# The second weight 32 bytes further in the on-chip memory

## The chip, the cores and the metric

The kernel runs on one core of a Trainium2 chip. A core has a matrix engine (PE; the loading of its stationary operand is shown as a row of its own, PEld), three engines that work on vectors (DVE, ACT and POOL), a queue engine (SP) that starts transfers, an on-chip memory of 128 partitions from which all engines read, and a small accumulation memory into which PE writes. The metric is the time of one execution in microseconds as the device reports it; lower is better. A time is the median of several executions.

## The reference

Two steps follow each other. The first is a windowed attention over 8 batches and 8 heads: 512 local positions that see 32 neighbours on either side and 32 global positions, and the 32 global positions that see everything.

```python
s_g = scale * np.matmul(q_g, k_all.transpose(0, 1, 3, 2))
out_g = np.matmul(sm(s_g), v_all)
mask = np.abs(pos[:, None] - pos[None, :]) <= window
s_ll = np.where(mask, scale * np.matmul(q_l, k_l.transpose(0, 1, 3, 2)), -1e9)
s_lg = scale * np.matmul(q_l, k_g.transpose(0, 1, 3, 2))
out_l = np.matmul(sm(np.concatenate([s_lg, s_ll], axis=-1)), np.concatenate([v_g, v_l], axis=2))
```

Its result, 4352 rows of 512 values, goes through a feed-forward layer with 2048 hidden values:

```python
h = x @ w_in
r = np.maximum(h, 0.0)
g = s * (r * r) + b
return (g @ w_out).astype(np.float32)
```

## The kernel before

Every float32 operand of a product is split into a rounded part and the rest, and a product is computed as three (rounded by rounded, rounded by rest, rest by rounded). So both weights lie in the on-chip memory twice, rounded part and rest: `wi` (line 109) and `wo` (line 110), each 65,536 bytes in every partition. They are loaded in 32 pieces at the start (`weight_piece`): a piece is decoded by ACT and DVE and written with one ACT copy (line 156, the rounded part) and one DVE subtraction (line 157, the rest).

The work is a loop over j. In round j the kernel computes the attention of head slot j (scores at line 355, the scores of the global positions at line 359, transposes at line 308, products with the values at line 380; now and then the global part at lines 428 and 451) and, ten rounds behind, one eighth of the feed-forward layer of 256 rows: `ffn_in` (line 499) and, a round later, `ffn_out` (line 532). There are 17 row tiles of 256 rows, so 136 such eighths. From j = 20 on the order of PE's instructions is the order in which the code stands.

An eighth is 24 products in `ffn_in`, each with a 128x128 piece of `wi` as the stationary operand and 256 columns of the tile `xs` as the moving operand, and 12 products in `ffn_out`, each with a 128x128 piece of the tile `g` as the stationary operand and 512 columns of `wo` as the moving operand:

```python
nc.tensor.matmul(
    oacc[t][i], lhsT=g[:, a, k, i * P:(i + 1) * P], rhs=wo[:, e, f, :],
    start=(pr == 0 and n == 0), stop=(pr == 7 and n == 5),
)
```

PE loads the stationary operand of the next product while the moving operand of the present one streams, so two reads of the on-chip memory go on at a time. Where the tiles lie is decided when the program is built. In bytes modulo 256, of the start in each partition:

| tile | role on PE | place modulo 256 before |
|---|---|---|
| `wi` | stationary, line 499 | 0 |
| `xs` | moving, line 499 | 32 |
| `g` (2 buffers) | stationary, line 532 | 0, 0 |
| `wo` | moving, line 532 | 0 |
| `kq` (3 buffers, used in turn) | stationary and moving, line 355 | 192, 224, 0 |
| `vs`, `pt` (2 buffers each) | stationary and moving, line 380 | 32 |

All pieces that PE reads of `wi`, `wo`, `g` and of the queries in `kq` start at a multiple of 512 bytes from the start of their tile, so they have the tile's place modulo 256.

Of the kernel before, what the change touches and what calls it, by code (L numbers as in the profile page):

```python
# [11 lines left out]
F32R = mybir.dt.float32r  # L12
# [8 lines left out]
DM, DF = 512, 2048  # L21
P = 128
# [45 lines left out]
def window_attention_then_ffn(ctx: ExitStack, tc: tile.TileContext, qd, qp, qg, kw, vw, vg, w_in, w_out, sv, bv, out):  # L68
# [3 lines left out]
    const = ctx.enter_context(tc.tile_pool(name="const", bufs=1))  # L72
# [34 lines left out]
        masks[first] = mask  # L107

    wi = const.tile([P, 2, 4, DF], F32R, name="wi")
    wo = const.tile([P, 2, 16, DM], F32R, name="wo")  # L110

    xg_d = dram.tile([B * SG, DM], F32, name="xg_d")

# [591 lines left out]
```

## Time and profile before

| | |
|---|---|
| median of 3 runs | 1034.99 us (1034.93 to 1036.73) |
| profiled execution, its own time | 1035.21 us |
| its span, first to last instruction | 1033.4 us |
| granted PE clock over the span | 0.979 |
| PE busy | 998.6 us (97%) |
| DVE, ACT, POOL busy | 813.8, 710.4, 300.2 us |
| line 499 (`ffn_in`) | 3264 products of 256 columns |
| line 532 (`ffn_out`) | 1632 products of 512 columns |

In the profile a PE row is a product, a PEld row the load of a stationary operand. Products are pipelined: the recorded duration of one is longer than the time from its start to the start of the next, and their ends are modelled, so durations of PE rows overlap. What a product costs is read from the starts, or from how its duration differs from that of another of the same shape.

### The profile page before, as it was taken

The page shows a single profiled execution, that of the slowest core. Times are in us where ns is not written, and L with a number is a line of the kernel's source. Part 1 is how long each engine was busy: PE and PEld are TensorE (multiplying, and loading weights), DVE is VectorE, ACT ScalarE, POOL GpSimd, SP SyncE. Part 2 cuts the span into 40 slices and gives each one's busy share as a digit, 9 for nine tenths or more (in the row PEclk, how much of TensorE's full clock was granted, in tenths as well). Part 3 has the DMA queues.
Part 4 walks back from the last instruction along what each step waited for, and adds up shares of the span by engine and source line. Part 5 has one row for each costly group of instructions (what it writes and reads, how often), then busy time and mean ns, then how long its engine had stood idle before and what let it go on. Part 6 is the DMA issues. An engine that isn't in the chain of part 4 may idle for free.

```text
span 1033.4 us, 20334 instructions
## 1 busy us (share of the span) xinstructions
PE 998.6 (97%) x7060; PEld 904.7 (88%) x7060; DVE 813.8 (79%) x2096; ACT 710.4 (69%) x1816; POOL 300.2 (29%) x365
## 2 busy tenths in 40 slices
PE   7779989999999999999999999999999999999996
PEld 3468879999999999999999999998999989999995
DVE  6999878888888988888888888888888888873321
ACT  6998767777676777777677777777677777643221
POOL 0000443333333433333323433344323433111000
PEclk8789989999999999999999999999999999999998
DMA  8764232222221222223221222222222321101000
GB/s 301 248 219 151 89 91 73 72 59 90 88 73 54 72 87 76 79 61 90 74 79 56 77 83 67 79 67 87 75 75 58 95 72 44 43 24 35 12 21 21
DMA packets 62254, 85.73 MB, mean 83 GB/s; under 512 B 7368, under 2 KB 49352, under 8 KB 62152
## 3 DMA queue, kind: packets, MB, share of 16 engines
q1 hardware_dynamic: 61864, 83.39, 26.1%
q8 instruction: 56, 0.92, 0.4%
q10 hardware_dynamic: 288, 1.05, 0.3%
q14 instruction: 46, 0.38, 0.1%
HBM read 74.97 MB, written 9.44 MB: 82 GB/s over the span
## 4 chain that ended last, share of the span: by engine, by line
PE 85%; ACT 5%; DVE 5%; DMA 3%; issue 1%; SPq 0%; DVEq 0%; ACTq 0%
PE ps_h L499 34%; PE acc L532 34%; PE ps_t L308 5%; PE ps_o L380 4%; PE ps_s L355 4%; PE ps_og L451 2%; DMA wst<-in_w_out 2%; PE ps_g L359 1%; ACT sm L219 1%; ACT wst L147 1%; DVE g L514 1%; DVE x L393 1%; DMA b_t<-in_bv 1%; DVE r L506 1%; ACT g L513 1%
## 5 line engine op out<-in xcount | busy, mean ns | idle before, releaser
L499 PE MATMUL ps_h<-xs,wi 128*128 128x256 f32 x3264 | 419.3, 284 | 0.0
L532 PE MATMUL acc<-wo,g 128*128 128x512 f32 x1632 | 405.0, 395 | 0.5 <-ACT g L513 0.5
L499 PEld LDWEIGHTS ps_h<-xs,wi 128*128 128x128 f32 x3264 | 397.1, 190 | 3.3 <-issue 0.5
L532 PEld LDWEIGHTS acc<-wo,g 128*128 128x128 f32 x1632 | 294.9, 188 | 56.8 <-ACT g L513 0.8
L514 DVE SCALAR_TENSOR_TENSOR g<-r,b_t,g 128x512 fp32r<-128x512 f32 x136 | 120.3, 885 | 57.6 <-ACT g L513 57.0
L505 ACT ACTIVATE r<-ps_h 128x512 f32<-128x512 f32 x136 | 81.3, 598 | 115.5 <-PE ps_h L499 109.7
L513 ACT ACTIVATE g<-r,b_t 128x512 fp32r<-128x512 f32 x136 | 98.4, 723 | 78.6 <-DVE r L506 78.1
L192 POOL TENSOR_TENSOR kq<-rq,kq 128x256 fp32r<-128x256 f32 x112 | 83.9, 750 | 231.1 <-ACT kq L191 226.7
L506 DVE SCALAR_TENSOR_TENSOR r<-ps_h,s_t,r 128x512 f32<-128x512 f32 x136 | 101.2, 744 | 58.3 <-ACT r L505 58.3
L190 POOL TENSOR_TENSOR kq<-rk,kq 64x416 fp32r<-64x416 f32 x56 | 61.0, 1089 | 264.3 <-ACT kq L189 254.4
L219 ACT ACTIVATE sm<-sm,nm 128x224 f32<-128x224 f32 (+1 forms) x256 | 119.7, 469 | 1.4 <-DVE nm L213 1.0
L200 POOL TENSOR_TENSOR vs<-rv,vs 128x256 fp32r<-128x256 f32 x112 | 91.2, 815 | 51.2 <-ACT vs L199 45.9
L308 PE MATMUL ps_t<-ident,sm 128*128 128x128 f32 (+1 forms) x512 | 96.8, 277 | 7.9 <-DVE pg L433 3.0
L363 ACT COPY tg<-ps_g 32x256 f32<-32x256 f32 (+1 forms) x112 | 42.3, 378 | 72.3 <-PE ps_g L359 71.7
L380 PE MATMUL ps_o<-pt,vs 128*128 128x256 f32 x448 | 91.0, 285 | 0.0
L213 DVE CUSTOM_DVE_ANT_0 sm<-ps_s,mask 128x192 f32<-128x192 f32 (+1 forms) x224 | 74.6, 370 | 11.2 <-PE ps_s L355 11.0
L443 POOL TENSOR_TENSOR vsg<-rvg,vsg 128x320 fp32r<-128x320 f32 x64 | 57.8, 924 | 77.5 <-ACT vsg L442 77.5
L391 DVE TENSOR_TENSOR u<-ps_o,u 128x256 f32<-128x256 f32 x112 | 47.3, 422 | 41.8 <-ACT u L390 40.0
L355 PE MATMUL ps_s<-kq 128*128 128x192 f32 (+1 forms) x448 | 78.4, 266 | 0.0
L355 PEld LDWEIGHTS ps_s<-kq 128*128 128x128 f32 x448 | 72.0, 190 | 6.8
L308 PEld LDWEIGHTS ps_t<-ident,sm 128*128 128x128 f32 (+1 forms) x512 | 58.4, 145 | 13.3 <-ACT ptp L315 4.6
L228 DVE TENSOR_SCALAR sm<-sm,ss 128x192 f32<-128x192 f32 (+1 forms) x224 | 68.0, 346 | 1.0
(83 smaller groups left out, 1239.2 us busy)
## 6 DMA issues: line engine op xcount, KB each, us to landing
rq<-in_qd SPq DMA_DIRECT2D x112, 128.0 KB, 2.3
rv<-in_vw SPq DMA_DIRECT2D x112, 128.0 KB, 2.1
rk<-in_kw SPq DMA_DIRECT2D x56, 208.0 KB, 2.4
rvg<-in_vg SPq DMA_DIRECT2D x32, 320.0 KB, 2.9
out<-o SPq DMA_DIRECT2D x34, 256.0 KB, 2.0
wst<-in_w_in SPq DMA_DIRECT2D x15, 512.0 KB, 4.3
wst<-in_w_out SPq DMA_DIRECT2D x15, 512.0 KB, 4.3
rvp<-in_vw SPq DMA_DIRECT2D x8, 256.0 KB, 3.5
```

Of the source, the lines that this page charges most:

```text
L192: nc.gpsimd.tensor_sub(out=qs[:, 1, :], in0=rq, in1=f32(qs[:, 0, :]))
L200: nc.gpsimd.tensor_sub(out=vs[:, :, 1, :], in0=rv4, in1=f32(vs[:, :, 0, :]))
L219: nc.scalar.activation(out=p, in_=p, func=AF.Exp, bias=nm[:, n:n + 1], scale=-1.0, accum_out=ss[:, n:n + 1],)
L308: nc.tensor.transpose(out=p_t[:, at:at + q], in_=sm[0:q, c0:c0 + P], identity=ident[0:q, 0:q])
L355: nc.tensor.matmul(p_s[:, cols], lhsT=qs[:, a, blk * P:(blk + 1) * P], rhs=ks[:, cols], start=(a == 0), stop=(a == 1),)
L380: nc.tensor.matmul(p_o[:, blk, :, q0:q0 + n], lhsT=vs[:, 2 * blk + c], rhs=pt[:, :, o], start=(c == 1), stop=(c == 0),)
L499: nc.tensor.matmul(p_h[:, k], lhsT=wi[:, a, c, f * P:(f + 1) * P], rhs=xs[:, e, c, :], start=(n == 0), stop=(n == 11),)
L505: nc.scalar.activation(out=r, in_=p_h, func=AF.Relu)
L506: nc.vector.scalar_tensor_tensor(out=r, in0=p_h, scalar=s_t, in1=r, op0=ALU.mult, op1=ALU.mult)
L513: nc.scalar.activation(out=g[:, 0], in_=r, func=AF.Identity, bias=b_t)
L514: nc.vector.scalar_tensor_tensor(out=g[:, 1], in0=r, scalar=b_t, in1=f32(g[:, 0]), op0=ALU.add, op1=ALU.subtract,)
L532: nc.tensor.matmul(oacc[t][i], lhsT=g[:, a, k, i * P:(i + 1) * P], rhs=wo[:, e, f, :], start=(pr == 0 and n == 0), stop=(pr == 7 and n == 5),)
```

## The change

`wo` is taken as 32 * 512 + 64 elements instead of 32 * 512, and its view starts 8 elements (32 bytes) into that.

```diff
-    wo = const.tile([P, 2, 16, DM], F32R, name="wo")
+    wo = const.tile([P, 32 * DM + 64], F32R, name="wo")
+    wo = wo[:, 8:32 * DM + 8].rearrange("p (a f d) -> p a f d", a=2, f=16)
```

In the built program `wo` itself now starts at 32 modulo 256. All tiles that are placed behind it (`kq`, `xs`, `g` and the rest) move by 256 bytes, so they keep their places modulo 256; `wi` and what lies before it do not move at all. The instructions of all five engines and the semaphores that they wait for stand in the same order as before, row by row. `ffn_in` and `ffn_out` read and compute the same values.

## The prediction

> **What bounds the kernel now.** I read the page's busy times and the chain of waits first, then the busy times by stretch.
>
> ```profile
> PE 998.6 (97%) x7060; PEld 904.7 (88%) x7060; DVE 813.8 (79%) x2096; ACT 710.4 (69%) x1816; POOL 300.2 (29%) x365
> PE 85%; ACT 5%; DVE 5%; DMA 3%; issue 1%; SPq 0%; DVEq 0%; ACTq 0%
> PE ps_h L499 34%; PE acc L532 34%; PE ps_t L308 5%; PE ps_o L380 4%; PE ps_s L355 4%; PE ps_og L451 2%; DMA wst<-in_w_out 2%; PE ps_g L359 1%; ACT sm L219 1%; ACT wst L147 1%; DVE g L514 1%; DVE x L393 1%; DMA b_t<-in_bv 1%; DVE r L506 1%; ACT g L513 1%
> 413.00:517.00 104.00, 103.50 (x762) 96.17 (x761) 87.73 (x234) 75.90 (x202) 38.09 (x45) 1.00 0.26 76
> L499 PE MATMUL ps_h<-xs,wi 128*128 128x256 f32 x3264 | 419.3, 284 | 0.0
> L532 PE MATMUL acc<-wo,g 128*128 128x512 f32 x1632 | 405.0, 395 | 0.5 <-ACT g L513 0.5
> ```
>
> The fourth row is a stretch of the steady stage: PE busy 103.5 of 104 us at the full granted clock (1.00), DVE 87.7, ACT 75.9, POOL 38.1. PE is the bound, the two feed-forward lines are two thirds of the chain, and L532, the only line that reads `wo` on PE, hardly ever waits (0.5 us in all). The next engine, DVE, has 16 us in 104 free. So whatever a product of L532 gets longer or shorter, up to many times what is in question here, goes into the end of the program one to one.
>
> How long is a product? The timeline of PE near the end, where no attention is left, shows it:
>
> ```profile
> 1004.82 2.96 PE L499 MATMUL ps_h<-xs,wi 128*128 128x256 f32 x24
> 1007.62 2.91 PE L532 MATMUL acc<-wo,g 128*128 128x512 f32 x12
> 1010.37 2.96 PE L499 MATMUL ps_h<-xs,wi 128*128 128x256 f32 x24
> ```
>
> The 12 products of L532 take 1010.37 - 1007.62 = 2.75 us, 229 ns each. Their recorded durations, first five and last seven of the same run:
>
> ```profile
> L532 PE MATMUL acc<-wo,g 128*128 128x512 f32 x5 | 1.3, 393 | 0.0
> L532 PE MATMUL acc<-wo,g 128*128 128x512 f32 x7 | 1.7, 389 | 0.0
> ```
>
> The mean is (5 x 393 + 7 x 389) / 12 = 390.7 ns, so a recorded duration is the true pace plus some 161 ns, and differences between durations are differences in pace. The five vary, and the last seven are equal:
>
> ```profile
> L532 PE MATMUL acc<-wo,g x5: 389/393/398, 1007.6 to 1008.5; 128*128 128x512 f32 x5
> L532 PE MATMUL acc<-wo,g x7: 389/389/389, 1008.8 to 1010.1; 128*128 128x512 f32 x7
> ```
>
> So the same instruction on the same kind of data takes 389 to 398 ns, with no other engine in the way: after some unsettled products the run falls into a quiet state at 389 (a pace of 227) and stays there. An ordinary product of L532 now has a mean of about 391 (another run, in the steady stage, shows the same); the 395 of the whole line holds the few that follow a wait or a transpose.
>
> ```profile
> L532 PE MATMUL acc<-wo,g 128*128 128x512 f32 x11 | 2.7, 390 | 0.0
> ```
>
> **The change part by part.** No instruction is added, removed or moved, and no wait. What remains is where bytes lie.
>
> First, the loads: the 16 ACT copies and 16 DVE subtractions into `wo` write at another place. The same two instructions into `wi` are the nearest rows:
>
> ```profile
> L157 DVE TENSOR_TENSOR wo<-we,wo 128x512 fp32r<-128x512 f32 x16 | 10.9, 688 | 1.0 <-ACT wo L156 1.0
> L157 DVE TENSOR_TENSOR wi<-we,wi 128x512 fp32r<-128x512 f32 x15 | 10.2, 683 | 0.0
> L156 ACT CAST wo<-we 128x512 fp32r<-128x512 f32 x16 | 9.8, 620 | 2.6 <-DVE we L152 2.5
> L156 ACT CAST wi<-we 128x512 fp32r<-128x512 f32 x15 | 9.3, 617 | 0.1
> ```
>
> These engines took no notice of which weight it was (5 and 3 ns apart). I take nothing; even 5 ns on all 32 with no cover is 0.16 us, either sign.
>
> Second, the tiles behind `wo` move by 256 bytes. Where two of them meet on PE their distance stays; towards `wi`, which does not move, it changes by 256. That everything depends on places modulo 256 at most is an assumption; I take nothing here and leave the failure to the range.
>
> Third, the term that matters: 1632 products read `wo` from 32 instead of 0 modulo 256 while the next piece of `g`, at 0, is loaded. Does PE care how the moving and the stationary operand lie to each other? The trace of before holds an experiment on it. At the end of most eighths, the last product of L532 streams `wo` (at 0) while the first stationary operand of L355 is loaded from one of the three `kq` buffers, at 0, 192 or 224 modulo 256. There are 37 such ends for each buffer. First and last of the 37, the duration of that one product, for the buffer at 0, then 192, then 224:
>
> ```profile
> L532 PE MATMUL acc<-wo,g x1: 389/389/389, 112.3 to 112.3; 128*128 128x512 f32 x1
> L532 PE MATMUL acc<-wo,g x1: 389/389/389, 894.4 to 894.4; 128*128 128x512 f32 x1
> L532 PE MATMUL acc<-wo,g x1: 388/388/388, 117.5 to 117.5; 128*128 128x512 f32 x1
> L532 PE MATMUL acc<-wo,g x1: 388/388/388, 901.3 to 901.3; 128*128 128x512 f32 x1
> L532 PE MATMUL acc<-wo,g x1: 397/397/397, 125.7 to 125.7; 128*128 128x512 f32 x1
> L532 PE MATMUL acc<-wo,g x1: 396/396/396, 908.2 to 908.2; 128*128 128x512 f32 x1
> ```
>
> A stationary operand at 224 costs the product 7 to 8 ns over one at 0 or 192. And 224 is 32 below the next 256: the moving operand lies 32 past the stationary one, modulo 256. That is exactly how `wo` at 32 will lie to `g` at 0, for every pair of products in `ffn_out`. So the first estimate is an ordinary mean of 396 instead of 391: 1632 x 5 ns = 8.2 us.
>
> What it does not tell is how the next product goes on. A product that took longer starts the next at another moment, and the unsettled rows above show that this matters. If the offset only takes the quiet state away, a product costs what the unsettled ones do now, 393 by the five of that run: 1632 x (393 - 391) = 3.3 us. I take the middle, 394.5: 1632 x 3.5 ns = **5.7 us**.
>
> Bounds on the other side: if the new offset has a quiet state too and a run falls into it at once, every ordinary product takes 388 to 389: 1632 x 2 to 3 ns, a gain of 3.3 to 4.9 us.
>
> Nearest to the new pairing in another shape is L499, moving operand `xs` at 32 against `wi` at 0:
>
> ```profile
> L499 PE MATMUL ps_h<-xs,wi x24: 277/279/283, 1004.8 to 1007.5; 128*128 128x256 f32 x24
> L499 PE MATMUL ps_h<-xs,wi x3264: 274/280/582, 46.0 to 1018.6; 128*128 128x256 f32 x192
> ```
>
> It settles, but at 279 to 280, while the line's fastest is 274 ns, 5 below its median. L532 with its operands at 0 and 0 settles at 389, over a minimum of 387. That speaks, weakly, for a dearer settled state at the new offset: 3 to 5 ns dearer than 389 is 392 to 394, 1.6 to 4.9 us in all. It is weak, since in L499 a load of the same size has half as long to hide.
>
> The Trainium skill says the opposite. "SBUF — State Buffer", section "Who interferes with whom", gives PE two independent read ports, one for the moving operand and one for the loading of weights, and says that PE and ACT never wait on anyone; by it the sum is nothing and the time stays 1035.2 us. The trace disagrees: the three buffers give 389, 388 and 396 ns in the same position.
>
> The sum: 1035.2 (the profiled execution, span 1033.4 and 1.8 around it) + 5.7 = 1040.9, say 1041 us. The median of the runs shown is 0.2 us below the profiled execution, which is less than the estimate can tell.
>
> **The rivals.**
>
> Rival A, no change. The runs of `ffn_out` unsettle and settle as they do now, only at another moment: the mean stays within 1 ns of 391, under 1.7 us. For it: the 12 products start from whatever L499 left, and already now a run is a mixture. Against: 7 ns in the one pairing that was tried, nearly every time. Time 1035, up to 2 us either way. The page named above would have this outcome too, by another reason.
>
> Rival B, faster. With `wo` at 32 against `g` at 0, L532 gets the same offset between its operands as L499, so that going from one line to the other no longer unsettles the run: every product at 388 to 389, the first five too. For it: the unsettled products stand at the start of a run, just behind L499. Against: the 396 at this offset. Time 1035.2 - 3.3 to 4.9, about 1031.
>
> Rival C, slower still: each product pays the full price of the pairing seen, 396 to 397, and never settles: 1632 x 5 to 6 ns = 8 to 10 us, 1043 to 1045. It is my own case at its end, and stands inside it.
>
> That the change doesn't do what it says can be left out: the built program has `wo` at 32.
>
> **How the numbers follow.** Slower, with C: 0.55. No change: 0.2. Faster: 0.25, as the pairing was seen only for one product after another offset, and a quiet state at the new one is quite possible. Less than 0.2% (2 us) can't be told from no change. The likeliest case by itself is 1038 to 1045. The range reaches to the faster rival, since that has a quarter: 1031 to 1045.
>
> **What would show it.** In the profile after, the median of L532 tells it: 393 to 397 with me, 389 with no change, 389 with a mean under 393 for the whole line with rival B. The row of L499 should stay at 284, since its operands keep their places modulo 256; if it moves, that assumption was wrong. The last product before L355 should change partners: slow with the `kq` buffer at 0 (moving 32 past stationary), quick with the one at 224. I am wrong if the 12 products settle within two or three of a start, at 389 or less.

## The result and the profile after

The change makes the kernel slower: the median goes from 1034.96 us (6 runs, 1034.61 to 1036.73) to 1040.66 us (6 runs, 1040.00 to 1043.00), a ratio of 1.0052 with a 95% interval of 1.0039 to 1.0065. The profiled execution took 1040.02 us, with a span of 1038.2 us against 1033.4, 4.8 us more.

Busy times, the steady stretch and the two feed-forward lines of the changed kernel (its lines stand one further down: 500 is 499 of before, 533 is 532):

```profile
PE 1004.9 (97%) x7060; PEld 905.1 (87%) x7060; DVE 814.7 (78%) x2096; ACT 710.0 (68%) x1816; POOL 300.7 (29%) x365
413.00:517.00 104.00, 103.57 (x753) 95.41 (x752) 87.98 (x234) 75.09 (x199) 37.27 (x44) 1.00 0.25 76
L500 PE MATMUL ps_h<-xs,wi 128*128 128x256 f32 x3264 | 419.8, 284 | 0.0
L533 PE MATMUL acc<-wo,g 128*128 128x512 f32 x1632 | 410.9, 398 | 0.8 <-ACT g L514 0.8
```

PE is busy 6.3 us longer, and 5.9 of that is in line 533 (405.0 before). DVE, ACT and POOL are within 1 us of before, line 500 is where it was (419.3 and 284 ns), and the granted clock is 1.00 in the stretch in both. The products of `ffn_out` alone have become longer.

A run near the end shows how. Timeline of PE of the changed kernel, then the distribution (shortest, median, longest) of the durations of products 6 to 11 of one run, first in the changed kernel (line 533) and then in the kernel before (line 532):

```profile
1009.51 2.96 PE L500 MATMUL ps_h<-xs,wi 128*128 128x256 f32 x24
1012.32 2.96 PE L533 MATMUL acc<-wo,g 128*128 128x512 f32 x12
1015.12 1.09 PE L500 MATMUL ps_h<-xs,wi 128*128 128x256 f32 x8
L533 PE MATMUL acc<-wo,g x6: 393/395/397, 1002.3 to 1003.4; 128*128 128x512 f32 x6
L532 PE MATMUL acc<-wo,g x6: 389/389/389, 1003.2 to 1004.4; 128*128 128x512 f32 x6
```

The 12 products take 1015.12 - 1012.32 = 2.80 us, 233 ns each in place of 229. The six that stood at 389 before now differ from neighbour to neighbour: from start to start the run goes 234, 231, 235, 233, 234, 231, 235, ... ns to its end. The quiet state at 227 ns has gone, and not in this run alone: in the trace of before, 98 of the 136 runs come to four neighbours within 2 ns of each other, at 226 to 227; in the trace after, none does. For the whole line:

```profile
L533 PE MATMUL acc<-wo,g x1632: 388/396/505, 70.8 to 1029.0; 128*128 128x512 f32 x182
L500 PE MATMUL ps_h<-xs,wi x3264: 274/280/583, 45.6 to 1023.4; 128*128 128x256 f32 x192
```

The median went from 389 to 396. Reading every start of the line from the two traces, and leaving out the some 70 products that follow a wait or a transpose (over 245 ns), the mean time from start to start is 229.5 ns before and 233.2 after: 3.7 ns more on 1560 products, 5.8 us. The intervals of the line as a whole, waits and all, add up to 380.4 us before and 385.5 after.

### The profile page after: what moved, and what is told of

Read it like the earlier page. It is cut to its first block, busy times and chain, and to the rows that moved or that the text cites. A ratio compares the mean times of both kernels' runs of the same rounds, so it can differ in the third digit from the quotient of the medians.

```text
span 1038.2 us, 20334 instructions
## 1 busy us (share of the span) xinstructions
PE 1004.9 (97%) x7060; PEld 905.1 (87%) x7060; DVE 814.7 (78%) x2096; ACT 710.0 (68%) x1816; POOL 300.7 (29%) x365
## 4 chain that ended last, share of the span: by engine, by line
PE 81%; DVE 8%; ACT 5%; DMA 3%; issue 2%; ACTq 0%; DVEq 0%
PE acc L533 33%; PE ps_h L500 33%; PE ps_t L309 4%; PE ps_o L381 4%; PE ps_s L356 4%; DMA wst<-in_w_out 2%; PE ps_og L452 1%; DVE g L515 1%; DMA wst<-in_w_in 1%; ACT sm L220 1%; PE ps_g L360 1%; DVE x L394 1%; DVE sm L229 1%; DVE r L507 1%; ACT wst L148 1%
## 5 line engine op out<-in xcount | busy, mean ns | idle before, releaser
L533 PE MATMUL acc<-wo,g 128*128 128x512 f32 x1632 | 410.9, 398 | 0.8 <-ACT g L514 0.8
L515 DVE SCALAR_TENSOR_TENSOR g<-r,b_t,g 128x512 fp32r<-128x512 f32 x136 | 119.8, 881 | 57.6 <-ACT g L514 57.2
L193 POOL TENSOR_TENSOR kq<-rq,kq 128x256 fp32r<-128x256 f32 x112 | 83.9, 749 | 232.8 <-ACT kq L192 228.3
```

The source lines that it names most:

```text
L193: nc.gpsimd.tensor_sub(out=qs[:, 1, :], in0=rq, in1=f32(qs[:, 0, :]))
L515: nc.vector.scalar_tensor_tensor(out=g[:, 1], in0=r, scalar=b_t, in1=f32(g[:, 0]), op0=ALU.add, op1=ALU.subtract,)
L533: nc.tensor.matmul(oacc[t][i], lhsT=g[:, a, k, i * P:(i + 1) * P], rhs=wo[:, e, f, :], start=(pr == 0 and n == 0), stop=(pr == 7 and n == 5),)
```

## The experiments

In all of them the instructions of every engine stand in the same order as in the kernel before, and the values computed are the same; only places in the on-chip memory differ. The edits are shown by their main lines; declarations and loads that go with them are left out. Ratios are taken against executions of the kernel before that were measured beside each experiment (medians 1034.20 to 1035.77 us). "Pace" is the time from the start of a product to the start of the next, in ns, read from the trace; products that follow a wait or a transpose are left out of its means.

Two theories were to be told apart. **R**: what counts is how the moving and the stationary operand lie to each other, modulo 256 (their distance). **M**: what counts is where the moving operand itself lies.

### The 256 bytes alone

```diff
-    wo = const.tile([P, 2, 16, DM], F32R, name="wo")
+    wo = const.tile([P, 32 * DM + 64], F32R, name="wo")
+    wo = wo[:, 0:32 * DM].rearrange("p (a f d) -> p a f d", a=2, f=16)
```

> The second weight takes the 256 bytes more, but its view starts at byte 0, so it stays at 0 modulo 256 and only the tiles behind it move by 256 bytes. If the offset of 32 costs the time (my theory), this is the kernel before: 1035 us, median duration of a product of ffn_out 389 ns, mean of the line 395. If the move of everything behind the weight by 256 bytes costs it (rival), this is the changed kernel: 1040 us, median 396.

Measured: 1035.15 us, 1.0010 of before (0.9997 to 1.0023), no change.

```profile
L533 PE MATMUL acc<-wo,g x1632: 387/390/504, 72.3 to 1024.8; 128*128 128x512 f32 x182
L533 PE MATMUL acc<-wo,g 128*128 128x512 f32 x1632 | 404.9, 395 | 0.0
```

The line's mean is 395 as before, and the pace 229.4. That everything behind the weight moved by 256 bytes costs nothing that can be measured; the 32 bytes do.

### Eight offsets in one kernel

With one place for each of the eight eighths of a row tile, one execution tries eight offsets, about 140 products each. First the moving operand is moved, then the stationary one, then both.

```diff
+    def wo_at(e, f):
+        o = e * (16 * DM + 64) + f * DM + 8 * (f // 2)
+        return wo[:, o:o + DM]
-                        oacc[t][i], lhsT=g[:, a, k, i * P:(i + 1) * P], rhs=wo[:, e, f, :],
+                        oacc[t][i], lhsT=g[:, a, k, i * P:(i + 1) * P], rhs=wo_at(e, f),
```

> The second weight lies at 0, 32, 64, ... 224 modulo 256, another one for each of the eight eighths of a row tile, g at 0. All theories: the eighths at 0 are as before (last seven products of a run at 389 ns), those at 32 as after (a mean of 394 to 396 without a settled value). If 32-byte steps matter modulo 64, the eighths at 32, 96, 160, 224 are all slow and those at 0, 64, 128, 192 all quick, and the time is half way, 1037 to 1038 us. If the modulus is 256, only one or a few of the eight are slow: 1035 to 1037 us.

```diff
+        go = 8 * (m % 8)
+        g = sb.tile([P, 4 * HALF + 64], F32R, tag="g", name=f"g{m}")[:, go:go + 4 * HALF]
```

> The second weight lies at 0 as before, and the tile g, the stationary operand, at 0, 32, ... 224 modulo 256, another one for each eighth. Theory R (what counts is how moving and stationary operand lie to each other): the eighths with g at odd multiples of 32 are slow, 394 to 396 ns, 1037 to 1038 us in all. Theory M (what counts is where the moving operand itself lies, whatever the stationary one does): all eight eighths are quick, 389 ns when settled, 1035 us.

The third has both edits.

> The second weight and g are moved together, by 0, 32, ... 224, another value for each eighth, so that they always lie equally. Theory R: all eighths are quick, settled at 389 ns, 1035 us. Theory M: the eighths at odd multiples of 32 are slow, 394 to 396 ns, 1037 to 1038 us.

Measured, one execution each: 1040.20 us with `wo` moved, 1039.72 with `g` moved, 1034.36 with both, against a median of 1034.20 of the kernel before on the same chip. Single executions of that kernel lay between 1032.51 and 1037.56 there, so from these kernels, and from the single executions further down, it is the paces that count and not the times. Mean pace of a product of `ffn_out`, by the distance of the moving from the stationary operand modulo 256 (some 140 products for each; taken over all products, the means move by at most 0.5 ns):

| moving minus stationary | 0 | 32 | 64 | 96 | 128 | 160 | 192 | 224 |
|---|---|---|---|---|---|---|---|---|
| `wo` moved | 230.0 | 233.6 | 229.1 | 233.9 | 232.2 | 234.3 | 233.1 | 233.1 |
| `g` moved | 229.9 | 232.8 | 229.7 | 234.2 | 232.4 | 234.1 | 233.5 | 233.1 |

The two rows agree within 0.8 ns, though in one the moving operand lies at eight places and in the other always at 0. An eighth of a row tile that has the distance 32 in the first kernel has 224 in the second, so it is not which eighth it is that sets the pace. With both moved the distance is always 0, and the pace is 228.0 to 230.1 at all eight places; the kernel before, with all at 0, has much the same spread over its eighths, 228.1 to 230.9. One run of each kernel, products 6 to 11; first `wo` at 32 and `g` at 0, then `wo` at 0 and `g` at 224, then both at 32, then both at 96:

```profile
L537 PE MATMUL acc<-wo,g x6: 393/395/397, 996.9 to 998.1; 128*128 128x512 f32 x6
L534 PE MATMUL acc<-wo,g x6: 393/395/397, 985.2 to 986.4; 128*128 128x512 f32 x6
L539 PE MATMUL acc<-wo,g x6: 389/389/389, 991.2 to 992.4; 128*128 128x512 f32 x6
L539 PE MATMUL acc<-wo,g x6: 389/389/390, 1002.3 to 1003.5; 128*128 128x512 f32 x6
```

The first two rows have the same distance, 32, and the same 393/395/397; the others have distance 0. R holds among the multiples of 32, and M falls. My number for the whole missed in both sweeps with one operand moved: I had expected half of the eighths or more to be quick, and only distance 0 has the quiet state. Of the others 64 is nearly as quick without one (its products go round 226, 229 and 232), and the rest stand at 232 to 234. Hence 1040 us where I had written 1037 to 1038.

### The change kept, the distance taken back

The changed kernel, with `g` moved by 32 bytes as well, in all eighths:

```diff
+        go = 8
+        g = sb.tile([P, 4 * HALF + 64], F32R, tag="g", name=f"g{m}")[:, go:go + 4 * HALF]
```

> The changed kernel, with g at 32 modulo 256 too in all eighths: the change is kept and only the offset between the two operands is taken back. Theory R (the offset between moving and stationary operand, modulo 256): the time of before, 1034 to 1035 us, median of ffn_out 389 ns. Theory M (the place of the moving operand itself): the time of after, 1040 us, median 395 ns.

Measured: 1034.79 us, 0.9988 of before (0.9976 to 1.0001). One of the 12 executions took 5292 us, which nothing here explains; it is not in the ratio, and the median of the other 11 is 1034.57.

```profile
L535 PE MATMUL acc<-wo,g x1632: 387/389/504, 71.4 to 1021.1; 128*128 128x512 f32 x182
L535 PE MATMUL acc<-wo,g 128*128 128x512 f32 x1632 | 405.3, 395 | 0.0
```

The whole loss is undone with the weight still at 32. The cause of the 5.7 us is the distance between the two operands that PE reads at a time.

### The same in `ffn_in`

```diff
+        xo = 8 * (t % 8)
+        xs = sb.tile([P, 8 * HALF + 64], F32R, tag="xs", name=f"xs{t}", bufs=1)[:, xo:xo + 8 * HALF]
```

> In ffn_in the moving operand xs lies at 32, 64, ... 224, 0 modulo 256 against wi at 0, another place for each of eight row tiles in turn. If ffn_in follows the same rule as ffn_out, the row tiles with xs at 0 are quickest, at the pace of 113 to 114 ns a product in place of 117 (duration 276 in place of 279), and the others at 115 to 117. If ffn_in is held by the loading of its stationary operand instead, all row tiles have the pace of 117. In all within 1.5 us of before either way, since two of 17 row tiles would gain 0.7 us each.

Measured: 1036.86 us, one execution. Mean pace by distance, moving minus stationary:

| 0 | 32 | 64 | 96 | 128 | 160 | 192 | 224 |
|---|---|---|---|---|---|---|---|
| 119.8 | 116.7 | 117.2 | 119.8 | 119.1 | 118.7 | 116.1 | 118.3 |

Here my expectation was wrong in both versions: the distance counts, so the loading is not a fixed bound, but 0, the best in `ffn_out`, is the slowest, together with 96. The 32 that the kernel has is the second best of the eight. And one distance does not have one pace. Products 9 to 23 of three runs of this kernel: two at distance 192 that follow each other in the program (the later one first), then one at distance 0:

```profile
L503 PE MATMUL ps_h<-xs,wi x15: 276/276/276, 870.2 to 871.8; 128*128 128x256 f32 x15
L503 PE MATMUL ps_h<-xs,wi x15: 281/281/281, 863.2 to 864.9; 128*128 128x256 f32 x15
L503 PE MATMUL ps_h<-xs,wi x15: 283/283/283, 501.8 to 503.5; 128*128 128x256 f32 x15
```

At 192 a run settles at 276 ns (a pace of 113.3) or at 281 (117.7), and then keeps to it for the rest of its 24 products; 6 of the 16 runs at 192 are of the first kind.

### Steps of four bytes

The second weight at 0, 4, ... 28 (the edit of the first sweep, with `f // 2` in place of `8 * (f // 2)`):

> The second weight lies at 0, 4, 8, ... 28 bytes past a multiple of 256, another place for each of the eight eighths, g at 0. If the memory serves blocks of 32 bytes or more, all eight are as at 0, settled at 389 ns, 1035 us. If the distance in bytes counts, the pace rises from 227 ns at 0 towards 234 at 28, evenly or from one point on, about 1037 to 1039 us.

Measured: 1037.95 us, one execution. Paces at 0, 4, 8, ... 28 bytes: 229.8, 235.7, 233.8, 229.0, 231.5, 237.9, 233.5, 228.2. It is neither of the two that I had expected: single elements count, and up and down rather than evenly. At 20 bytes a run can stay at 240 ns, the slowest state of all.

### All 64 distances, and a search

```diff
+        go = m % 64
+        xo = 16 * (t % 4)
-                        p_h[:, k], lhsT=wi[:, a, c, f * P:(f + 1) * P], rhs=xs[:, e, c, :],
+                        p_h[:, k], lhsT=wi[:, a, c, f * (P + 1):f * (P + 1) + P], rhs=xs[:, e, c, :],
```

> All 64 offsets in steps of 4 bytes at once: g lies at 4 * (m modulo 64) bytes against the second weight at 0, another place for each eighth m, and in ffn_in the piece f of wi lies at 4 * f bytes against xs at 32, 96, 160, 224 by row tile. If the pace depends on the offset alone, modulo 256, the multiples of 32 repeat what the earlier runs showed (ffn_out: 227 settled at 0, 229 at 64, 232 to 234 at the others; ffn_in: 116 to 117 at 32 and 192, 118 to 120 at the others), and the time is 1037 to 1042 us. It is open whether any of the other offsets is quicker than 227 in ffn_out or than 116 in ffn_in; by the 4-byte steps seen so far (228 to 240) I expect none under 226 and 113.3, which are 17/16 of the columns at 2.4 columns a ns.

Measured: 1042.66 us, one execution. In `ffn_out` two of the 64 distances, 0 and 136, settled at 226.7 to 227.0 ns in more than one of their two or three runs, and none below (one early run at 240 and one at 124 got there as well); 136 did so from the second product on, in both of its runs. In `ffn_in` distance 204 settled at 113.3 to 113.8 in all four of its runs, 168 and 88 in three of four (32, the kernel's own: 117.4). So I tried 136 and 204 on the whole kernel, by moving what was easiest to move, `wo` and `xs`:

```diff
-    wo = const.tile([P, 2, 16, DM], F32R, name="wo")
+    wo = const.tile([P, 32 * DM + 64], F32R, name="wo")
+    wo = wo[:, 34:32 * DM + 34].rearrange("p (a f d) -> p a f d", a=2, f=16)
```

> The second weight at 136 modulo 256 in all eighths, g at 0: the offset at which the run with all 64 was settled at 227 ns from the second product on. If the offset alone decides, ordinary products go from 229.5 to about 227 ns: 1560 x 2.5 ns = 3.9 us less, 1031 us. Rival (which state a run falls into hangs on what precedes it, and two runs of 12 are no proof): between 1033 and 1037 us.

```diff
+        xo = 43
+        xs = sb.tile([P, 8 * HALF + 64], F32R, tag="xs", name=f"xs{t}", bufs=1)[:, xo:xo + 8 * HALF]
```

> Only xs is moved, to 204 modulo 256 against wi at 0; ffn_out as before. If the offset alone decides, a run of 24 products is settled at 113.4 ns after five or six at 117: 3264 x 2.2 ns = 7 us less, 1028 us. Rival: as at 192, where about half of the runs stay at 118, it gains half of that or less, 1031 to 1034 us.

> Both of these: the second weight at 136, xs at 204. If the two add up, 11 us less than before, 1024 us, 1.1% faster; if vector work takes over as the bound, less than the sum of the two.

Measured: 1041.26 us (1.0050, 1.0033 to 1.0067), 1038.88 us (1.0029, 1.0018 to 1.0041) and 1044.23 us (1.0075, 1.0061 to 1.0090). All three are slower, where the theory had forecast gains of up to 1.1%, and no rival a loss of more than 1.3 us. `ffn_out` has a pace of 234.4 with `wo` at 136, `ffn_in` 118.2 with `xs` at 204. Beside the run of the sweep at the same distance of 136 (made there with `wo` at 0 and `g` at 120), this is the run with `wo` at 136 and `g` at 0, products 6 to 11:

```profile
L538 PE MATMUL acc<-wo,g x6: 389/389/389, 297.2 to 298.4; 128*128 128x512 f32 x6
```

```profile
L533 PE MATMUL acc<-wo,g x6: 395/395/395, 1003.7 to 1004.8; 128*128 128x512 f32 x6
```

Same distance, two settled states, 6 ns apart. Off the multiples of 32, the distance alone doesn't decide: with the moving operand at 136 and at 204 the quick states of the sweep, which had kept it at multiples of 32, were not to be had.

The last run makes the same two distances as the sweep did, with the moving operands at 0 and 224 and the stationary ones moved:

```diff
+    wi = wi[:, 5:8 * DF + 5].rearrange("p (a c f) -> p a c f", a=2, c=4)
+        xo = 48
+        go = 30
```

> The same two offsets as in the run before, 136 in ffn_out and 204 in ffn_in, but made as in the run with all 64: the moving operands stay at multiples of 32 (the second weight at 0, xs at 224) and the stationary ones are moved (g to 120, wi to 20). Theory P (both the offset and the place of the moving operand in its block count): ffn_out at 227 ns from the second product on and ffn_in at 113.4 after five or six, 1024 to 1027 us. Theory H (which state a run falls into hangs on what precedes it, and the short runs at these offsets were chance): no better than before, 1035 to 1042 us, ffn_in at 118.

Measured: 1032.00 us, 0.9968 of before (0.9956 to 0.9981): 0.3% faster than the kernel before, and so faster than both. First a run of `ffn_out`, then three runs of `ffn_in` that follow each other and one of its last 16 (products 9 to 23):

```profile
L539 PE MATMUL acc<-wo,g x6: 389/389/389, 996.2 to 997.3; 128*128 128x512 f32 x6
L504 PE MATMUL ps_h<-xs,wi x15: 276/276/276, 429.7 to 431.3; 128*128 128x256 f32 x15
L504 PE MATMUL ps_h<-xs,wi x15: 282/283/284, 436.6 to 438.2; 128*128 128x256 f32 x15
L504 PE MATMUL ps_h<-xs,wi x15: 276/276/276, 443.5 to 445.1; 128*128 128x256 f32 x15
L504 PE MATMUL ps_h<-xs,wi x15: 279/281/284, 987.6 to 989.3; 128*128 128x256 f32 x15
```

P holds for `ffn_out`: the quiet state is there, 124 of the 136 runs reach it (98 before), and the pace falls from 229.5 to 227.9. For `ffn_in` H is as right: 66 of its 136 runs stand at 113.3 from the ninth product on and 88 from the thirteenth; nearly all the others go on at 118 to 120, and the mean is 116.3 against 117.0. The last 16 runs of the program come after the end of the local attention, where the product before a run is one of `ffn_out`, and all 16 go on at 118; 109 of the 120 runs before them follow a transpose of the attention. That speaks for what comes before a run, though no experiment changed that alone. In all it gained 3.4 us by the medians where P had said 8 to 11. In the profiled execution, the slowest of the six with 1033.8 us, the intervals of `ffn_out` add up to 1.9 us less than before and those of `ffn_in`, the waits included, to no less; of the 3.4 us, the trace shows 1.9.

## Why the prediction was right

**What bounds.** PE stayed the bound and no other engine took over; the intervals of `ffn_out` add up to 5.1 us more, and the span is 4.8 us longer. One to one, as said.

**The loads and the 256 bytes at nothing.** Right: with the 256 bytes alone the ratio is 1.0010 (0.9997 to 1.0023). Line 500 kept its 284 ns.

**The term, 1632 x 3.5 ns = 5.7 us.** It measured 3.7 ns on 1560 ordinary products, 5.8 us, less 0.7 us in the products behind waits. I had taken the middle between the full price of the pairing seen before (396, 8.2 us) and the unsettled products of before (393, 3.3 us). What it became is a cycle of its own: 231, 235, 233, 234 ns, a mean of 233.3 (a duration of 395), without end and without a settled value. That the change would take the quiet state away is what happened; that the mean would fall in the middle was a choice between two bounds, not derived. The mechanism was read from the trace, but that the sum came within 1 us (5.7 against 4.8 in the span and 5.1 in the line) is in part luck.

**The evidence from the three `kq` buffers** was read rightly as to its cause, the distance between the two operands: the sweeps showed it with either operand moved. It did not carry everything it could have: at 192 (distance 64) the trace of before has 388, and the sweep confirms 64 as nearly quick, 229, though with no settled value.

**The Trainium skill's rule** ("SBUF — State Buffer", "Who interferes with whom": two independent read ports, PE never waits on anyone) would have given 1035.2 us. The trace disagrees in all sweeps: the pace of one and the same product is 227 to 240 ns by the distance of its operands. Whether it is the ports that meet, or something behind them, no run here shows.

**The rivals.** A (no change) and B (a new quiet state, faster) did not come. B's reason, that an equal distance in both lines would spare the unsettled start of a run, falls: in the kernel after both lines have distance 32, and `ffn_out` is unsettled throughout. B was not idle as a thought, since quiet states at other distances exist (136), but not at 32. C, each product at 396 to 397, was 1 to 2 ns too dear.

**The signs named ahead.** The median of 393 to 397 came as 396. The change of partners came in part only. The last product before the first score, for the `kq` buffer at 0, 192 and 224, one from the middle of the kernel each:

```profile
L533 PE MATMUL acc<-wo,g x1: 393/393/393, 508.7 to 508.7; 128*128 128x512 f32 x1
L533 PE MATMUL acc<-wo,g x1: 396/396/396, 515.7 to 515.7; 128*128 128x512 f32 x1
L533 PE MATMUL acc<-wo,g x1: 388/388/388, 522.7 to 522.7; 128*128 128x512 f32 x1
```

The buffer at 0 became slow (393 to 397 in all 37, before 389 in 33 of them), as said, and the one at 224 quicker, but only to a median of 393: 25 of its 37 stand there, and the 388 shown is one of 6. A likely reason is that the run before it is no longer quiet; no run tests it.

## What to carry to other kernels

Where PE is the bound and the stationary operand of the next product is loaded while the present one streams, the places of the two operands are a parameter of some per cent of a product: lay tiles that PE reads together at an equal place modulo 256 first if the products have 512 columns, but measure, since with 256 columns the equal place was among the slowest. Read it from the start-to-start times of single products; a mean hides that a run either settles or doesn't. And a quick state found in a short run at a mixed layout is no forecast for a whole kernel: two of mine came back at the very places at which they had been seen and not in the one other layout tried, and one of them only in two thirds of the runs.

## What was not expected of the hardware

- A run of equal products is a sequence with a memory. It starts unsettled and falls into one of several states, which it keeps: 226.7 ns, 233.3, or 240 for 512 columns, and 113.3, 116.7, 117.7 or 120, among others, for 256. In both shapes three of them stand to each other as 34, 35 and 36 (226.7, 233.3, 240; 113.3, 116.7, 120). Why is open.
- The distance counts in steps of one element of 4 bytes (229.8, 235.7, 233.8, 229.0 ns at 0, 4, 8, 12 bytes), and its best value is another one for 512 columns (0) than for 256 (192 and 32 among the multiples of 32).
- Off the multiples of 32 the distance alone does not decide: 389 ns and 395 ns are settled values at the same distance of 136, the one with the moving operand at 0 and the stationary one at 120, the other with them at 136 and 0. Whether it is the place of the moving or of the stationary operand in a smaller block, or what the run before left, was not separated.
